# Attention's small products moved to TensorE's full tile size, with a new cost rule in the order planner

## The chip, the core and the metric

One core of one Trainium2 chip runs the whole program. The metric is the device time of one execution in microseconds (us). TensorE is the matrix engine (PE in the profile; its weight loads are listed apart, as PEld), DVE is VectorE, ACT is ScalarE, POOL is GpSimd, and SP issues most DMA transfers.

## The reference

Three layers follow each other; all data are float32.

```python
p_packed = sm_attn(p, k, v)          # 8 batches x 8 heads, 32 packed queries over 576 keys of 64
out = sm_attn(q, p_packed, p_packed) # 576 queries over the 32 packed rows
x = out.transpose(0, 2, 1, 3).reshape(4608, 512)
logits = x @ w_gate                  # 8 experts
# greedy: the largest logits first; each token goes to one expert, each expert takes 576 tokens
out[mask_e] = relu(x[mask_e] @ w1[e]) @ w2[e]
# then, for all tokens:
y = maximum(maximum(x @ w1, x @ w2), x @ w3) @ w_out
```

## The kernel before

The program has two parts. Each collects its operations in an `Order` object and then lets `run` write them out in an order that a planner works out with its own costs (`price`) and its own clock per engine. The planner always takes the operation that can start first; at equal start the lower `level` wins, then the earlier one collected. So the order on each engine's queue is fixed at build time; the chip follows it with semaphores. When the planner sees TensorE idle it calls `busy`, which puts dummy bf16 products (L562) in the gap: `int((us - GAP) * FILL / 0.22)` of them.

**Part one, attention.** For each of 8 batches `load` fetches keys (kt), values (v4, and the last 64 keys' values in v1), packed queries (pt) and queries (qt). Inside `pack`, for each of two groups of four heads: the packed logits `s` (stationary 128 rows x 64 columns), softmax, five transposes of `a1` (the fifth has 64 columns only), the product with the values into 32-row pieces (stationary 32 columns; the last chunk has only 64 contraction rows), two transposes, and `G`, the gate weights pulled through the packed values (stationary 64 columns). `query` then takes one or two tiles of 128 tokens: logits in pieces of 64 tokens (L521 to L523), softmax on DVE and ACT, transposes, and the gate logits in pieces of 32 tokens (L552 to L555) into `Lm`. `attend` multiplies the softmax with the block-diagonal packed values and stores a tile of 128 rows of x to memory (`x_dram`). Nine of the 36 tiles are attended in part one, 27 in part two.

A float32 product is recorded as two instructions on TensorE, so every count of such products in the profile is twice that of the code. The shape of the array that an instruction uses follows its operands: `128*64` in the profile is 128 contraction rows by 64 stationary columns, and products of a shape under 128 run side by side on different parts of the array.

`some` converts a piece of the last layer's weights from 64-bit words (`raw64`, `c64`, `w64`, `both64`) and writes it back to memory. It runs at level 30, that is, only where the planner finds nothing else to do. There are 18 pieces; 7 are collected into part one, the other 11 into part two (4 ahead of `gather(0)`, 7 later; all of them at level 30 and through the same two buffers).

**Part two, experts.** `epoch(k)` finds on DVE, with small products on TensorE, which expert fills next and which 576 tokens it takes (`idx`). `gather(k)` fetches their rows of `x_dram` with POOL's indirect DMA; it waits for the stores of all of x. Then the expert layers and the last layers follow for those tokens on TensorE. `epoch(0)` and the 27 attends come first; `epoch(k+1)` is planned beside expert k.

## Time and profile before

| what | value |
|---|---|
| median of 3 runs | 1273.7 us (1271.32 to 1274.76) |
| the profiled execution's own time | 1274.22 us |
| its span, first to last instruction | 1272.5 us |
| PE busy, share of the span | 1225.9 us, 96% |
| PEld busy | 1138.2 us, 89% |
| DVE busy | 778.4 us, 61% |
| ACT busy | 380.2 us, 30% |
| mean granted TensorE clock | 0.980 |
| one load of qt, of v4, of v1 | 1152, 1024 and 128 KB |

Times inside the execution are microseconds from the span's start. Busy time of PE contains the latency of its pipeline: the number of instructions that start in a stretch says more than the busy share. PEclk is the granted clock as a share of 2.4 GHz.

### The profile page before, as it was taken

Reading aid. Unit: us, or ns where it says so; the run is one execution under the profiler, and the core shown is the slowest. Engines: PE = TensorE matmul, PEld = TensorE weight load, DVE = VectorE, ACT = ScalarE, POOL = GpSimd, SP = SyncE. Lnnn points to the kernel's source line nnn. Section 1 sums busy time; section 2 is a strip of 40 time slices with the busy share of each in tenths; the row PEclk is TensorE's granted clock in tenths of the full one; section 3 lists DMA queues with packets and bytes.
Section 4 is the critical chain, followed back from the end, with each engine's and each line's share of the span. In section 5 each row is a group of like instructions: output and inputs, shape, how many; then the busy total and the mean of one; then the engine's idle time right before and its main releaser. Section 6 shows DMA issues by size and latency. Waiting matters only on the chain.

```text
span 1272.5 us, 25973 instructions
## 1 busy us (share of the span) xinstructions
PE 1225.9 (96%) x10396; PEld 1138.2 (89%) x10396; DVE 778.4 (61%) x2129; ACT 380.2 (30%) x849; POOL 85.2 (7%) x221
## 2 busy tenths in 40 slices
PE   8999877999899999999999999999999999999997
PEld 4667767999799989999999989998999899989995
DVE  4879789999889999999993522252225222432220
ACT  3445445334321233123312422133213221332121
POOL 1000001000301020001100020002000300010001
PEclk9999897999899999999999999999999999999999
DMA  9984485884426433443244224433443345323511
GB/s 342 363 317 166 152 275 187 261 273 130 133 85 214 120 114 99 134 142 108 91 149 157 85 100 142 151 97 117 142 153 98 114 133 166 92 75 100 166 34 42
DMA packets 70058, 191.50 MB, mean 150 GB/s; under 512 B 7729, under 2 KB 17969, under 8 KB 67889
## 3 DMA queue, kind: packets, MB, share of 16 engines
q1 hardware_dynamic: 63712, 169.89, 41.2%
q0 software_dynamic: 6080, 19.93, 4.7%
q8 instruction: 82, 1.34, 0.4%
q14 instruction: 40, 0.32, 0.1%
q10 hardware_dynamic: 144, 0.02, 0.0%
HBM read 161.50 MB, written 28.31 MB: 149 GB/s over the span
## 4 chain that ended last, share of the span: by engine, by line
PE 58%; issue 16%; DVE 4%; POOL 1%; DMA 1%; ACT 0%; POOLq 0%; DVEq 0%; ACTq 0%
PE mm L190 57%; POOL out_dram L867 1%; DMA xg<-x_dram,idx 1%; DVE R L190 1%; PE pst L190 1%; PE psr L190 1%; DVE act L190 0%; DVE t L190 0%; DVE hl L190 0%; DVE eq L190 0%; DVE val L190 0%; DVE m L190 0%; DVE pj L190 0%; DVE pos L190 0%; POOL xg L190 0%
## 5 line engine op out<-in xcount | busy, mean ns | idle before, releaser
L190 PE MATMUL mm<-act,hl 128*128 128x288 f32 x6528 | 886.4, 297 | 0.7 <-ACT act L190 0.6
L190 PEld LDWEIGHTS mm<-act,hl 128*128 128x128 f32 x6528 | 874.3, 189 | 2.1 <-ACT act L190 1.4
L190 DVE TENSOR_TENSOR t<-mm,t 128x288 f32<-128x288 f32 x192 | 87.5, 456 | 143.4 <-PE mm L190 143.1
L190 ACT ACTIVATE act<-mm 128x288 fp32r<-128x288 f32 (+1 forms) x208 | 81.4, 398 | 239.7 <-PE mm L190 233.8
L190 PE MATMUL mm<-WO,act 128*128 128x512 f32 x576 | 144.4, 401 | 0.0
L190 PEld LDWEIGHTS mm<-WO,act 128*128 128x128 f32 x576 | 103.9, 188 | 22.9
L190 ACT ACTIVATE hl<-raw 128x512 fp32r<-128x512 f32 x128 | 80.7, 633 | 120.0 <-PE mm L190 101.3
L190 DVE TENSOR_TENSOR hl<-raw,hl 128x512 fp32r<-128x512 f32 x128 | 87.6, 690 | 45.8 <-ACT hl L190 42.5
L190 ACT ACTIVATE act<-t 128x288 fp32r<-128x288 f32 x96 | 42.6, 443 | 208.9 <-DVE t L190 208.2
L190 DVE SCALAR_TENSOR_TENSOR act<-mm,act 128x288 fp32r<-128x288 f32 x128 | 58.0, 454 | 69.4 <-ACT act L190 69.2
L190 POOL DMA_INDIRECT xg<-x_dram,idx x40 | 41.4, 1035 | 701.2 <-PE pst L190 449.8
L190 DVE TENSOR_TENSOR act<-mm,act 128x288 fp32r<-128x288 f32 (+1 forms) x80 | 32.6, 422 | 88.6 <-ACT act L190 88.6
L190 ACT ACTIVATE osb<-mm 128x512 f32<-128x512 f32 x63 | 37.1, 599 | 120.4 <-PE mm L190 113.1
L867 POOL DMA_INDIRECT out_dram<-osb,idx x32 | 33.8, 1057 | 465.4 <-ACT osb L190 285.0
L190 DVE TENSOR_REDUCE ri<-R 128x30 int32<-128x1080 bf16 x48 | 61.2, 1275 | 0.8
L190 DVE TENSOR_TENSOR act<-t,act 128x288 fp32r<-128x288 f32 x96 | 43.8, 456 | 23.2 <-ACT act L190 23.0
L190 ACT ACTIVATE t<-mm 128x288 f32<-128x288 f32 x96 | 39.2, 409 | 57.5 <-PE mm L190 56.7
L190 DVE TENSOR_TENSOR R<-m,cand 128x540 bf16<-128x540 f32 (+1 forms) x63 | 36.3, 594 | 0.0
L190 DVE TENSOR_TENSOR R<-R,code 128x1080 bf16<-128x1080 bf16 x48 | 34.6, 720 | 0.9
L190 PE MATMUL mm<-act 128*128 128x128 f32 (+1 forms) x240 | 34.2, 301 | 0.9 <-DVE Lm L190 0.9
L190 PE MATMUL s<-kt,pt 128*64 128x288 f32 x128 | 29.4, 440 | 3.2 <-ACT a L190 3.2
L190 DVE TENSOR_TENSOR act<-pst,act 128x64 fp32r<-128x64 f32 (+1 forms) x60 | 24.2, 438 | 13.3 <-ACT act L190 13.1
(157 smaller groups left out, 910.7 us busy)
## 6 DMA issues: line engine op xcount, KB each, us to landing
hl<-W SPq DMA_DIRECT2D x144, 512.0 KB, 4.0
raw<-in_w_dram SPq DMA_DIRECT2D x128, 256.0 KB, 2.7
kt<-in_kT_dram SPq DMA_DIRECT2D x16, 576.0 KB, 8.5
qt<-in_qT_dram SPq DMA_DIRECT2D x8, 1152.0 KB, 9.8
raw<-in_w_dram SPq DMA_DIRECT2D x18, 512.0 KB, 5.9
W<-both SPq DMA_DIRECT2D x18, 512.0 KB, 4.7
v<-in_v_dram SPq DMA_DIRECT2D x8, 1024.0 KB, 9.7
x_dram<-osb SPq DMA_DIRECT2D x27, 256.0 KB, 4.3
```

The lines of the kernel that those rows point to most:

```text
L190: return self.add(eng, aps, cost, moved, lambda: getattr(engine, method)(*args, **kw), after)
L867: ins = nc.gpsimd.indirect_dma_start(out=out, out_offset=bass.IndirectOffsetOnAxis(ap=idx, axis=0), in_=osb, in_offset=None)
```

## The change

The queries' logits take all rows of a tile in one product (stationary up to 128 columns instead of 64); the gate logits do too (128 instead of 32). `G` is one product for both pairs of heads, with 16 moving columns, from which ScalarE copies the two useful blocks; before, two products and one DVE copy. The fifth transpose of `a1` takes the last 128 columns, so that the last value product has 128 contraction rows; the 64 rows that repeat are met by zeros that POOL writes into the lower half of v1. Three buffers for queries and values instead of two. The conversion pieces are collected per batch, 6 in place of 7 in part one and 5 in place of 4 ahead of `gather(0)` (18 in all, as before).

In the planner, a float32 product gets a new price, each change of the array's shape on TensorE costs 0.15 us, and at equal start and level the operation that needs no such change goes first. The gap filler takes smaller gaps and more of each. In `epoch`, `pd` and `val` are computed ahead of `nb`, `r` and `R1`.

```diff
-QTB = KTB = 2
-UNITS_A, UNITS_B = 7, 4
+QTB, KTB, VB = 3, 2, 3
+UNITS_A, UNITS_B = (0, 0, 1, 2, 2, 1, 0, 0), 5
-GAP, FILL = 0.6, 0.7
+GAP, FILL = 0.4, 0.8
+SWITCH = 0.15
...
-                return 4 * max(cols, k) / self.PE_SPEED * min(1.0, k / 128) * (1.12 if k < 128 else 1.0) + 0.022
+                wide = 32 if k <= 32 else 64 if k <= 64 else 128
+                return 2 * max(2 * cols, wide) / self.PE_SPEED * wide / 128 * (1.12 if k < 128 else 1.0) + 0.012
...
+    def turns(self, i):
+
+        return self.modes.get(i, self.mode) != self.mode
...
-                    can = sorted((s, ops[i][3], i) for i in c if (s := start(i)) is not None)
+                    can = sorted((s, (ops[i][3][0], self.turns(i), i), i) for i in c if (s := start(i)) is not None)
...
-            self.free[eng] = e = s + cost
+            self.free[eng] = e = s + cost + (SWITCH if self.turns(i) else 0.0)
+            self.mode = self.modes.get(i, self.mode)
...
-            V4[b] = o.tile(inp, [P, 4, DM], F32, "v4", 2)
+            V4[b] = o.tile(inp, [P, 4, DM], F32, "v4", VB)
             o.sp.dma_start(V4[b], v4[b])
-            V1[b] = o.tile(inp, [64, DM], F32, "v1", 2)
-            o.sp.dma_start(V1[b], v1[b])
+            V1[b] = o.tile(inp, [P, DM], F32, "v1", VB)
+            o.pool.memset(V1[b][:64], 0.0)
+            o.sp.dma_start(V1[b][64:], v1[b])
...
-                turn(t2[:64], a1[:, 512:])
+                turn(t2, a1[:, S - P:])
...
-                o.dve.tensor_copy(a1T[:64, 4], t2[:64])
+                o.dve.tensor_copy(a1T[:, 4], t2)
                 for c in range(5):
-                    w = min(P, S - c * P)
...
-                        o.pe.matmul(pp[32 * h:32 * h + 32, :64], a1T[:w, c, 32 * h:32 * h + 32],
+                        o.pe.matmul(pp[32 * h:32 * h + 32, :64], a1T[:, c, 32 * h:32 * h + 32],
...
+                o.pe.matmul(pp[:, 320:320 + 2 * E], PPT[b][:, 2 * g:2 * g + 2].rearrange("p a c -> p (a c)"),
+                            wg_sb[:, 2 * g:2 * g + 2].rearrange("p a e -> p (a e)"), start=True, stop=True)
                 for pr in range(2):
-                    o.pe.matmul(pp[64 * pr:64 * pr + 64, 320:320 + E], PPT[b][:, 2 * g + pr], wg_sb[:, 2 * g + pr],
-                                start=True, stop=True)
-                o.dve.tensor_copy(G[:, b, g], pp[:, 320:320 + E])
+                    rows = slice(64 * pr, 64 * pr + 64)
+                    o.act.activation(G[rows, b, g], pp[rows, 320 + E * pr:320 + E * pr + E], AF.Copy)
...
-                        for c in range(0, m, 64):
-                            o.pe.matmul(ps[r0 + c:r0 + c + 64, i, 64 * pr:64 * pr + 64], QT[b][:, pr, tok + c:tok + c + 64],
-                                        PPT[b][:, pr], start=True, stop=True)
+                        o.pe.matmul(ps[r0:r0 + m, i, 64 * pr:64 * pr + 64], QT[b][:, pr, tok:tok + m], PPT[b][:, pr],
+                                    start=True, stop=True)
...
-                    for c in range(0, m, 32):
-                        for g in range(2):
-                            o.pe.matmul(pl[r0 + c:r0 + c + 32, i * E:(i + 1) * E], aT[b][:, g, tok + c:tok + c + 32],
-                                        G[:, b, g], start=(g == 0), stop=(g == 1))
+                    for g in range(2):
+                        o.pe.matmul(pl[r0:r0 + m, i * E:(i + 1) * E], aT[b][:, g, tok:tok + m], G[:, b, g],
+                                    start=(g == 0), stop=(g == 1))
...
-        o.level = 0
-        some(work, UNITS_A)
+            o.level = 0
+            some(work, UNITS_A[b])
```

In `epoch` the five lines that make `pd` and `val` move, unchanged, from behind the loop that makes `R1` to a place ahead of `nb`.

## Rows read from the trace of the kernel before

**Rows 1.** Stretches of the span: stretch, length, busy us and instructions of each engine.

```profile
core 0: us, PE busy (x) PEld busy (x) DVE busy (x) ACT busy (x) POOL busy (x), PEclk, DMA share, GB/s
25.00:77.00 52.00, 49.19 (x948) 33.88 (x948) 43.78 (x137) 22.98 (x47) 0.00 (x0) 1.00 1.02 365
77.00:125.00 48.00, 45.41 (x873) 33.31 (x874) 40.09 (x121) 22.16 (x45) 0.00 (x0) 0.96 0.64 220
125.00:138.00 13.00, 8.82 (x238) 6.87 (x234) 12.67 (x43) 5.50 (x11) 0.00 (x0) 0.84 0.11 43
138.00:179.00 41.00, 40.27 (x523) 36.72 (x524) 31.24 (x127) 18.04 (x32) 0.00 (x0) 0.93 0.67 232
...
331.00:341.00 10.00, 6.74 (x34) 4.28 (x33) 8.43 (x18) 3.00 (x5) 2.06 (x2) 0.89 0.27 101
```

**Rows 2.** Waits of the weight loads, 0 to 143 us: total us, times, longest.

```profile
PEld bank L190 <- issue: 15.7, 43, 1.8
```

**Rows 3.** Timeline of weight loads around 127 us: start, us, count, idle before.

```profile
126.61 0.42 PEld L190 LDWEIGHTS bank<-eye,a 128*128 128x128 f32 x4 [0.61 <-issue]
127.20 1.01 PEld L190 LDWEIGHTS bank<-ppt,qt 128*64 128x64 f32 x30 [0.17 <-issue]
128.27 0.38 PEld L190 LDWEIGHTS bank<-G,act 128*32 128x32 f32 x32
128.67 0.20 PEld L190 LDWEIGHTS bank<-ppt,qt 128*64 128x64 f32 x4
```

**Rows 4.** Groups of weight loads by shape, 0 to 146 us.

```profile
L190 PEld LDWEIGHTS bank<-ppt,qt 128*64 128x64 f32 x576 | 22.7, 140 | 5.6 <-issue 4.4
...
L190 PEld LDWEIGHTS bank<-G,act 128*32 128x32 f32 x576 | 8.3, 116 | 9.3 <-issue 4.7 <-ACT act L190 3.2 <-ACT e L190 0.6
...
L190 PEld LDWEIGHTS bank<-eye,a 128*64 128x64 f32 x16 | 1.8, 114 | 2.0 <-issue 1.3 <-DVE c L190 0.4 <-ACT a1T L190 0.2
```

**Rows 5.** Timeline: runs of full-width weight loads in three stages.

```profile
19.41 0.20 PEld L190 LDWEIGHTS bank<-eye,act 128*128 128x128 f32 x2 [0.44 <-DVE act L190]
...
162.95 0.97 PEld L190 LDWEIGHTS mm<-act 128*128 128x128 f32 x8
...
398.92 2.15 PEld L190 LDWEIGHTS mm<-act,hl 128*128 128x128 f32 x16
```

**Rows 6.** Groups of DVE instructions, 0 to 146 us: busy us, mean ns.

```profile
L190 DVE TENSOR_SCALAR c<-c 128x512 f32<-128x512 f32 (+1 forms) x14 | 5.8, 417 | 0.2 <-ACT c L190 0.2
L190 DVE SCALAR_TENSOR_TENSOR w<-raw,c 128x512 int32<-128x512 int32 x7 | 4.8, 686 | 0.0
...
L190 DVE COPY G<-bank 128x8 f32<-128x8 f32 x16 | 2.6, 159 | 3.6 <-PE bank L190 3.5
```

**Rows 7.** Groups of ACT instructions, 0 to 210 us.

```profile
L190 ACT ACTIVATE act<-pst 128x64 fp32r<-128x64 f32 x4 | 0.6, 232 | 0.7 <-PE pst L190 0.7
```

**Rows 8.** Timeline where part one ends, 138 to 146 us.

```profile
138.28 7.89 PEld L190 LDWEIGHTS mm<-act 128*128 128x128 f32 x48 [1.03 <-DVE Lm L190]
...
139.36 0.42 DVE L190 TENSOR_SCALAR c<-w 128x512 int32<-128x512 int32 x1
...
145.34 0.69 DVE L190 TENSOR_TENSOR both<-w,both 128x512 fp32r<-128x512 f32 x1 [0.70 <-ACT both L190]
145.95 0.42 DVE L190 TENSOR_SCALAR eq<-who 128x288 f32<-128x288 bf16 x1
```

**Rows 9.** Timeline of epoch 0's end and the gather, 183 to 191 us.

```profile
183.51 1.36 SPq L190 DMA_DIRECT2D x_dram<-osb  x3
...
185.04 0.53 DVE L190 TENSOR_TENSOR val<-tk,pd 128x360 bf16<-128x360 bf16 x1
...
185.62 0.76 PE L190 MATMUL psr<-val,R 128*128 128x40 bf16 x18 [4.53 <-DVE val L190]
...
187.45 0.16 DVE L190 CAST idx<-psr 128x5 int32<-128x5 f32 x1 [0.20 <-PE psr L190]
...
190.41 1.21 POOL L190 DMA_INDIRECT xg<-x_dram,idx  x1 [184.00 <-DMA raw<-in_w_dram]
```

More of the change, by code (lines that the diff above doesn't have):

```diff
@@ L75, in __init__ @@
         self.level, self.pe_level, self.filler = 0, None, None
+        self.mode = None
         self.free = dict.fromkeys(("pe", "dve", "act", "pool", "sp", "dma"), 0.6)
@@ L81, in reset @@
         self.ops, self.seen, self.touch = [], {}, {}
+        self.modes = {}
         self.queue_of = {}
@@ L189, in trace @@
             cost, moved = self.price(eng, method, aps, kw), 0
-        return self.add(eng, aps, cost, moved, lambda: getattr(engine, method)(*args, **kw), after)
+        me = self.add(eng, aps, cost, moved, lambda: getattr(engine, method)(*args, **kw), after)
+        if eng == "pe":
+            lhs = next(x for x, write in aps if not write)
+            self.modes[me] = tuple(32 if n <= 32 else 64 if n <= 64 else 128
+                                   for n in (int(lhs.shape[0]), int(np.prod([int(d) for d in lhs.shape[1:]]))))
+        return me
     @staticmethod
@@ L753, in epoch @@
                             op=OP.is_ge)
+        pd = T([P, NT, 10], BF, "pd")
+        o.dve.tensor_tensor(pd, pj[:, :, :10], pj[:, :, 1:], op=OP.subtract)
+        val = T([P, NT, 2, 5, 2], BF, "val")
+        for h in range(2):
+            o.dve.tensor_tensor(val[:, :, h], tk[:, :, None, :].to_broadcast([P, NT, 5, 2]),
+                                 pd[:, :, h:10:2][:, :, :, None].to_broadcast([P, NT, 5, 2]), op=OP.mult)
         nb = T([P, NT], F32, "nb")
@@ L760, in epoch @@
                                 r[:, c:c + 12, None].to_broadcast([P, 12, 64]), op=OP.is_equal)
-        pd = T([P, NT, 10], BF, "pd")
-        o.dve.tensor_tensor(pd, pj[:, :, :10], pj[:, :, 1:], op=OP.subtract)
-        val = T([P, NT, 2, 5, 2], BF, "val")
-        for h in range(2):
-            o.dve.tensor_tensor(val[:, :, h], tk[:, :, None, :].to_broadcast([P, NT, 5, 2]),
-                                 pd[:, :, h:10:2][:, :, :, None].to_broadcast([P, NT, 5, 2]), op=OP.mult)
         pi = R()
```

## The prediction

> **What bounds the kernel now.** I read the stretches of the span first, to see which engine sets each stage, then the waits, the timeline at the seams, and the groups for prices. From 25 to 125 us TensorE is busy 94.6 of 100 us, DVE 83.9, and the DMA engines are full only up to 77 us [rows 1]. But TensorE's busy time holds little work: its weight loads stand idle 15.7 us before products into a bank with nothing that the profile shows [rows 2]. The timeline says where: inside a run the loads follow closely, between runs of two shapes there is a hole [rows 3]. From 125 to 138 us DVE takes over: 12.67 of 13 us busy, while TensorE falls to 8.82 and its granted clock to a mean of 0.84 [rows 1]. From 138 us TensorE attends the 27 tiles that are left, at first slowly: 48 loads in 7.89 us [rows 8], 164 ns each, where the same loads later take (0.97 - 0.14) / 7 = 119 ns at most [rows 5]. DVE, meanwhile, finishes conversion pieces from 139.36 to 145.95 us before epoch 0 can begin [rows 8]. At the far end the token indices are there at 187.45 + 0.16 us, yet the gather starts at 190.41; the last three stores of x were issued at 183.51 to 184.87 [rows 9]. So the stores, behind TensorE's attends, come last there, and DVE's epoch 2.8 us before them. From there to the end the experts run on a full TensorE, which the change does not touch but through the planner.
>
> So what is to be gained is how much earlier the attends can start, and how fast they run.
>
> **The change part by part.**
>
> *Shape changes on TensorE.* Out of the four full-width transposes, the last load starts at about 126.61 + 0.42 - 0.14 = 126.89 us and the first 64-column load at 127.20: 0.31 us, against 0.11 within the run, so 0.20 us for the change. From 32 columns back to 64: 128.27 + 0.38 - 0.11 = 128.54 to 128.67, 0.13 us against 0.01, so 0.12 us [rows 3]. The Trainium skill, TensorEngine Tiling (Array Packing), Key Properties, has the reason: a change of tiling mode, not of tile, drains TensorE; it gives no price, the trace does. How many changes go: the 64-column transpose among full ones, 16 times in and out [rows 4] = 32; the value chunk of 64 rows, 16; the gate products, 16; from the code, 20 query calls whose logits and gate logits each go into a small shape and out, 80. That is 144 at most; where a small-shape neighbour stays (the packed logits `s`, the 32-column value products, the four tiles that straddle two batches) nothing is saved. I take 100 at 0.15 us: -15 us. Bounds: 60 x 0.12 = -7, 140 x 0.20 = -28.
>
> *Queries.* 32 of 36 tiles lie in one batch: 512 of the 576 loads become 256 of 128 columns. The old ones follow at (1.01 - 0.14) / 29 = 30 ns [rows 3]: 15.4 us. The trace has no full-width float32 load before 64 moving columns. From below: two full-width loads start 0.20 - 0.14 = 0.06 us apart [rows 5], which is also twice the 30 ns at which two half-width products run side by side. From above: 110 ns, the run of transposes and attends [rows 3, 5], which have 128 moving columns, twice as many. I take 65 ns, since the expert products show a load hidden under its predecessor's 288 columns at 134 ns [rows 5]: 16.6 us, +1.2 (0 to +12.8).
>
> *Gate logits.* 512 loads at (0.38 - 0.11) / 31 = 8.7 ns [rows 3] = 4.5 us become 128; at 65 ns 8.3 us, +3.8 (+3.2 to +9.6). Alone, this part loses; it pays only through its shape changes. `G` itself: 64 loads become 32, zero within 1 us either way.
>
> TensorE's net: -15 + 1.2 + 3.8 = -10 us, between -24 and +15.
>
> *DVE.* The copies of `G` go: 16 x 0.159 = -2.5 us. One piece fewer in part one: 2 x 0.417, four like the 0.686, one more like the first, -4.0 us [rows 6]. Conversion is collected batch by batch, but it keeps level 30 and its own buffers, and no other operation has that level: as far as I can see the spreading itself alters nothing in the plan, only the count does. The piece that goes to part two costs DVE 4.0 us there; it is covered by the 9.8 us that DVE idles between 138 and 179 us [rows 1] and by the 6.6 us of leftovers that no longer stand ahead of epoch 0. Uncovered it would be +4.
>
> *ACT and POOL.* 32 copies for `G`, nearest row 0.232 us [rows 7]: 7.4 us on an engine that is busy 45 of 100 us there [rows 1]; hidden, and 7.4 us on the path if every one were waited for. POOL's eight zero fills: no row is near; by DVE's 512 columns, 0.69 us each, 5.5 us as an upper estimate; POOL is idle from 25 to 179 us [rows 1] and the third buffer gives a batch of lead. Zero.
>
> *Third buffers.* Values and queries of batch 2, 2.3 MB, now go to SP's queue ahead of batch 2's keys, which at 365 GB/s [rows 1] come 6.3 us later. The batch is complete after the same number of bytes, and the queries then need not wait for a buffer. Zero, with up to +6 if DVE has nothing else then (it idles 8.2 us in 25 to 77 us as it is).
>
> *`val` ahead of `R1`.* The 18 products now wait 4.53 us for `val` [rows 9]; afterwards two thirds could run under the making of `R1`: at most 0.5 us, on a chain that the stores of x outlast. Zero.
>
> *Fillers.* More dummy products in smaller gaps keep the clock up over 125 to 138 us, unless they delay real ones. The slow 48 loads cost 48 x 0.054 = 2.6 us; I take half, -1.3.
>
> *Sum.* The attends start when the last gate logits are through, which DVE sets. It loses 2.5 us of work, and gets back part of its idle time, 16.5 us from 25 to 138 us, since the engine that it waits for is 10 us lighter: I take half of those 10. That is -7.4 us (0 to -12.5), and with the clock -8.7. The gather needs the attends' stores, so this passes through to the experts. Epoch 0 gains more (its leftovers go as well) and stays ahead. From 1274.2 us of the profiled execution, 1265.5; its time is 0.5 us above the median shown, so 1265.
>
> The experts' order is planned anew with shifted clocks. It has one soft place, 331 to 341 us, where TensorE is busy 6.74 of 10 us before expert 1's gather [rows 1]: +-3 us, taken as zero.
>
> **The rivals.**
>
> *The loads are not hidden.* Each full-width float32 load costs what it does in the attends, 110 ns. Then 384 loads take 42.2 us in place of 19.9, and less the 15 us of shape changes TensorE is 7.4 us heavier; DVE waits for it, and the time goes to about 1280. It decides from (15 + 19.9) / 384 = 91 ns a load. For it: no run in the trace is closer than that. Against: the pair 0.06 us apart. A rule speaks for this rival: the Trainium skill, TensorE: Matmul & The Clock Gate, LDWEIGHTS (loading the stationary operand), has a load take its columns over 1.2 in ns, 107 ns for 128 columns, whatever moves; by that I estimate 384 x 107 = 41 us and a time of 1279. The pair disagrees with it.
>
> *The gain is given back.* TensorE gets lighter but DVE, over 97% busy at the end of part one, starts the attends only its own 2.5 us earlier, or the epoch with its extra piece, or the new order at 331 us, eats the rest: 1271 to 1276. For it: DVE from 77 to 138 us is busy 52.8 of 61 us. Against: 8 us of that stretch are idle, and epoch 0 has 6.6 us of slack to come.
>
> *All of it counts.* DVE's idle time is all recovered, the clock holds, and the order at 331 us improves: 1274.2 - 12.5 - 2.6 - 3 = 1256.
>
> **How the numbers follow.** The forecast 0.61 (its own range 1258 to 1269), given back 0.21, loads not hidden 0.13, all of it 0.05. A measurement of this kernel tells about 0.3%, 3.8 us, from no change. So faster 0.66, same 0.21, slower 0.13. The range of 8 in 10 reaches from 1256 to 1277: below lies half of the last case, above the unhidden loads.
>
> **What would show it.** Right: the first attend near 131 us; full-width query loads 60 to 70 ns apart; the unexplained 15.7 us more than halved; DVE free of conversion when the last gate logits are copied; the gather near 182 us, and the expert part as long as before. Wrong: query loads 90 ns or more apart; the first attend at 138 us with DVE full up to it; a gather that waits for the indices in place of the stores; or a wider hole around expert 1's gather.

## The result and the profile after

| | median us | range | against the kernel before |
|---|---|---|---|
| before, beside it | 1274.08 | 1271.32 to 1274.76 (4 runs) | |
| changed | 1288.79 | 1286.96 to 1293.61 (4 runs) | 1.0125 [1.0094, 1.0157], slower by 1.2%, clear of noise |

The forecast was 1265 us, the range 1256 to 1277. The profile shown here is of the slowest of the four executions (1293.61 us, span 1291.8). Two of e13's ten executions ran in a slower state and are left out of its median below.

First the stretches of the changed kernel, in the columns of [rows 1]; from 138 us on the cuts follow its own stages.

```profile
core 0: us, PE busy (x) PEld busy (x) DVE busy (x) ACT busy (x) POOL busy (x), PEclk, DMA share, GB/s
25.00:77.00 52.00, 49.93 (x568) 39.72 (x564) 35.85 (x105) 23.48 (x55) 1.56 (x3) 0.93 0.97 349
77.00:125.00 48.00, 46.67 (x573) 36.89 (x571) 38.94 (x118) 21.07 (x51) 0.52 (x1) 0.93 0.54 193
125.00:138.00 13.00, 12.65 (x190) 11.17 (x189) 10.45 (x34) 5.58 (x16) 0.00 (x0) 1.00 0.11 42
138.00:150.00 12.00, 10.75 (x82) 8.32 (x81) 10.53 (x34) 5.00 (x10) 0.00 (x0) 0.98 0.12 46
...
339.00:361.00 22.00, 16.79 (x68) 12.66 (x68) 18.41 (x56) 5.09 (x12) 7.57 (x7) 0.69 0.39 131
```

From 25 to 125 us TensorE is busier than before (96.6 of 100 us against 94.6) with far fewer instructions (1138 against 1818 in the 100 us taken as one), and its weight loads rise from 67.2 to 76.6 us. DVE, which was to gain, falls from 83.9 to 74.8 busy us: its waits for TensorE in these 100 us rise from 14.5 to 23.4 us. The granted clock is lower too, 0.93 against 0.98. The last row is a hole of 22 us which before was a soft place of 10.

The timeline of the changed kernel's weight loads (start, us, count) gives the price that the forecast had to guess.

```profile
90.22 0.97 PEld L194 LDWEIGHTS bank<-ppt,qt 128*128 128x128 f32 x8
91.50 0.97 PEld L194 LDWEIGHTS bank<-G,act 128*128 128x128 f32 x8
...
130.76 0.97 PEld L194 LDWEIGHTS bank<-G,act 128*128 128x128 f32 x8 [0.15 <-ACT act L194]
131.65 0.97 PEld L194 LDWEIGHTS bank<-ppt,qt 128*128 128x128 f32 x8
```

Eight loads in 0.97 us, the last of them 0.19: (0.97 - 0.19) / 7 = 111 ns from load to load, for 64 moving columns (ppt) as for 8 (G). Between all neighbours of one run up to 158 us the median distance is 112 ns for the queries and 111 to 112 for the gate logits. None of the load time is hidden. This is the pace at the full clock; where the granted clock stood at the lower of its two levels (1.2 GHz), from 36.8 to 43.6 us, the same loads follow at 213 ns.

The groups of its weight loads, in the form of [rows 4], give the counts:

```profile
L194 PEld LDWEIGHTS bank<-ppt,qt 128*128 128x128 f32 x256 | 32.8, 200 | 1.0 <-issue 0.4
L194 PEld LDWEIGHTS bank<-G,act 128*128 128x128 f32 x128 | 16.3, 195 | 0.9 <-ACT act L194 0.8
```

256 x 0.112 = 28.7 us in place of the 15.4 of the 64-column loads, 128 x 0.112 = 14.3 in place of 4.5: TensorE pays 23 us. On the other side the unexplained waits of [rows 2] fall from 15.7 to 6.5 us (waits of the weight loads, 0 to 155 us):

```profile
PEld bank L194 <- issue: 6.5, 22, 0.9
```

In the sequence of the loads, the changes of the array's shape go from 176 (to 143 us, where part one ends) to 107 (to 160 us), and the distances from load to load across them, each counted up to 0.3 us, from 42.0 to 28.4 us. So TensorE gains 13.6 and pays 23.2: about 10 us heavier, where the forecast had it 10 us lighter.

The seam between the parts, on the timeline, as in [rows 8]:

```profile
150.38 7.89 PEld L194 LDWEIGHTS mm<-act 128*128 128x128 f32 x48 [0.43 <-DVE Lm L194]
151.46 0.68 DVE L194 TENSOR_TENSOR w<-w,c 128x512 f32<-128x512 f32 x1
...
156.29 0.69 DVE L194 TENSOR_TENSOR both<-w,both 128x512 fp32r<-128x512 f32 x1 [0.70 <-ACT both L194]
156.90 0.42 DVE L194 TENSOR_SCALAR eq<-who 128x288 f32<-128x288 bf16 x1
```

The attends start at 150.4 us (before: 138.3), DVE still has 5.5 us of conversion ahead of epoch 0, and the attends start as slowly as before, 48 loads in 7.89 us in both. In both the granted clock is at its lower level there, first the changed kernel, then the kernel before (stretches, in the columns above):

```profile
149.40:156.20 6.80, 6.47 (x31) 6.37 (x31) 5.32 (x15) 1.20 (x3) 0.00 (x0) 0.50 0.20 80
133.90:144.10 10.20, 8.85 (x113) 8.30 (x114) 9.70 (x32) 1.53 (x4) 0.00 (x0) 0.50 0.13 53
```

At epoch 0's end, as in [rows 9]:

```profile
194.48 0.85 SPq L194 DMA_DIRECT2D x_dram<-osb  x2
196.11 0.32 PE L194 MATMUL psr<-val,R 128*128 128x40 bf16 x6 [0.55 <-DVE R L194]
197.41 0.16 DVE L194 CAST idx<-psr 128x5 int32<-128x5 f32 x1
201.83 1.12 POOL L194 DMA_INDIRECT xg<-x_dram,idx  x1 [113.28 <-DMA W<-both]
```

The indices are ready at 197.57 and the gather starts at 201.83: the last store lands at 200.6, so as before it is the stores that come last, and the gather stands 11.4 us later than in [rows 9].

Expert 1's tokens then come later still. On the timelines of the kernel before (L190) and of the changed one (L194), DVE's copy that makes the indices and, right behind it, the gather:

```profile
322.72 0.16 DVE L190 CAST idx<-psr 128x5 int32<-128x5 f32 x1
323.15 1.18 POOL L190 DMA_INDIRECT xg<-x_dram,idx  x1 [1.13 <-DVE idx L190]
338.43 0.15 DVE L194 CAST idx<-psr 128x5 int32<-128x5 f32 x1
338.86 1.04 POOL L194 DMA_INDIRECT xg<-x_dram,idx  x1 [2.13 <-DVE idf L194]
```

Here it is the indices that come last, 15.7 us later than before. In the hole of the stretch 339 to 361 TensorE waits for the tokens, on the timeline:

```profile
347.59 0.37 PE L194 MATMUL pst<-eye,xg 128*128 128x128 f32 x1 [1.84 <-DMA xg<-x_dram,idx]
```

Expert 0's last layer starts 11.1 us later than before, expert 1's 19.2 later (475.4 against 456.2). From there to the end every kernel of this study takes 815 to 818 us. So all of the loss lies ahead of 476 us: the profiled executions differ by 1293.61 - 1274.22 = 19.4 us.

So two paths lead into the experts. The stores of x set expert 0. DVE's epochs, one behind the other, set expert 1: in all eighteen kernels expert 1's last layer starts 132 to 137 us behind its indices, though these come anywhere from 305 to 346 us, and the indices come 135 to 150 us behind expert 0's. From expert 0's last layer to expert 1's it is 134 to 136 us where there is hardly a hole (e3, e6, e9, e12, e13, e14), 142.4 in the kernel before and 150.5 in the changed one. A late epoch 0 therefore reaches the end even where, as at the first gather, the stores outlast it.

### The profile page after: what moved, and what is told of

Its sections match the earlier page's. It is cut to its first block, busy times and chain, and to the rows that moved or that the text cites. A ratio compares the mean times of both kernels' runs of the same rounds, so it can differ in the third digit from the quotient of the medians.

```text
span 1291.8 us, 24638 instructions
## 1 busy us (share of the span) xinstructions
PE 1249.3 (97%) x9712; PEld 1164.8 (90%) x9712; DVE 777.7 (60%) x2113; ACT 385.3 (30%) x881; POOL 88.0 (7%) x229
## 4 chain that ended last, share of the span: by engine, by line
PE 75%; issue 12%; DVE 9%; DMA 2%; POOL 1%; ACT 1%; POOLq 0%; DVEq 0%; ACTq 0%
PE mm L194 63%; PE bank L194 8%; PE s L194 2%; PE psr L194 1%; DVE R L194 1%; DMA xg<-x_dram,idx 1%; PE pst L194 1%; DVE act L194 1%; DVE c L194 1%; DVE t L194 1%; DVE hl L194 1%; POOL out_dram L880 1%; DMA raw<-in_wo_dram 1%; PE wp L575 0%; POOL xg L194 0%
## 5 line engine op out<-in xcount | busy, mean ns | idle before, releaser
L194 PE MATMUL mm<-act,hl 128*128 128x288 f32 x6528 | 893.0, 298 | 0.8 <-ACT act L194 0.7
L194 PEld LDWEIGHTS mm<-act,hl 128*128 128x128 f32 x6528 | 877.4, 189 | 2.7 <-ACT act L194 1.7
L194 DVE TENSOR_TENSOR t<-mm,t 128x288 f32<-128x288 f32 x192 | 87.3, 455 | 148.2 <-PE mm L194 147.1
L194 ACT ACTIVATE act<-mm 128x288 fp32r<-128x288 f32 (+1 forms) x208 | 81.2, 398 | 246.6 <-PE mm L194 246.4
L194 PE MATMUL mm<-WO,act 128*128 128x512 f32 x576 | 144.5, 401 | 0.0
L194 PEld LDWEIGHTS mm<-WO,act 128*128 128x128 f32 x576 | 104.1, 188 | 22.7
L194 ACT ACTIVATE hl<-raw 128x512 fp32r<-128x512 f32 x128 | 80.7, 632 | 125.3 <-PE mm L194 102.2
L194 DVE TENSOR_TENSOR hl<-raw,hl 128x512 fp32r<-128x512 f32 x128 | 87.7, 688 | 45.4 <-ACT hl L194 41.8
L194 ACT ACTIVATE act<-t 128x288 fp32r<-128x288 f32 x96 | 42.4, 442 | 215.5 <-DVE t L194 214.9
L194 DVE SCALAR_TENSOR_TENSOR act<-mm,act 128x288 fp32r<-128x288 f32 x128 | 57.9, 453 | 69.9 <-ACT act L194 69.9
L194 DVE TENSOR_TENSOR act<-mm,act 128x288 fp32r<-128x288 f32 (+1 forms) x80 | 32.5, 419 | 89.6 <-ACT act L194 89.4
L194 POOL DMA_INDIRECT xg<-x_dram,idx x40 | 40.9, 1022 | 635.7 <-PE pst L194 450.7
L194 ACT ACTIVATE osb<-mm 128x512 f32<-128x512 f32 x63 | 37.2, 598 | 115.4 <-PE mm L194 106.0
L194 DVE TENSOR_REDUCE ri<-R 128x30 int32<-128x1080 bf16 x48 | 61.1, 1273 | 0.8
L194 DVE TENSOR_TENSOR act<-t,act 128x288 fp32r<-128x288 f32 x96 | 43.6, 454 | 23.6 <-ACT act L194 23.5
L194 ACT ACTIVATE t<-mm 128x288 f32<-128x288 f32 x96 | 39.1, 407 | 55.5 <-PE mm L194 53.5
L194 PE MATMUL bank<-ppt,qt 128*128 128x64 f32 (+1 forms) x320 | 39.3, 277 | 0.0
L194 PEld LDWEIGHTS bank<-ppt,qt 128*128 128x128 f32 (+1 forms) x320 | 35.9, 191 | 1.9 <-issue 0.9
L194 DVE TENSOR_TENSOR R<-m,cand 128x540 bf16<-128x540 f32 (+1 forms) x63 | 36.2, 593 | 0.0
L194 DVE TENSOR_TENSOR R<-R,code 128x1080 bf16<-128x1080 bf16 x48 | 34.5, 719 | 0.9
L194 PE MATMUL mm<-act 128*128 128x128 f32 (+1 forms) x240 | 34.4, 301 | 0.3 <-DVE Lm L194 0.3
```

The lines of the kernel that those rows point to most:

```text
L194: me = self.add(eng, aps, cost, moved, lambda: getattr(engine, method)(*args, **kw), after)
```

## The experiments

Four theories were put against each other. A: the full-width loads take 112 ns each and nothing hides them. B: the planner prices a full-width float32 product at 0.119 us (it has two loads, so 0.224 on the chip) and puts the work into an order that counts on time that is not there. C: the pieces, the buffers or the shape rule. D: the third buffers delay batch 2's keys. "The kernel before" in each row ran beside the experiment.

| run | median us | ratio to the kernel before |
|---|---|---|
| e1_small_pieces | 1270.19 | 0.9966 [0.9952, 0.9979] |
| e2_full_tiles_alone | 1277.07 | 1.0025 [0.9998, 1.0053] |
| e3_true_price | 1279.06 | 1.0037 [1.0020, 1.0053] |
| e4_seven_pieces | 1295.77 | 1.0154 [1.0120, 1.0188] |
| e5_full_tiles_low_price | 1290.81 | 1.0133 [1.0113, 1.0153] |
| e6_small_two_buffers | 1265.20 | 0.9939 [0.9920, 0.9959] |
| e7_keys_and_gate_alone | 1269.48 | 0.9972 [0.9956, 0.9988] |
| e8_third_buffers_alone | 1281.11 | 1.0067 [1.0042, 1.0091] |
| e9_gate_logits_full | 1260.50 | 0.9914 [0.9895, 0.9933] |
| e10_queries_full | 1290.64 | 1.0142 [1.0110, 1.0174] |
| e11_no_shape_rule | 1280.32 | 1.0059 [1.0042, 1.0075] |
| e12_third_keys | 1266.66 | 0.9958 [0.9941, 0.9975] |
| e13_same_order_queries | 1268.89 | 0.9970 [0.9944, 0.9995] |
| e14_same_order_gate | 1267.60 | 0.9955 [0.9940, 0.9970] |
| e15_before_order_full | 1286.83 | 1.0117 [1.0073, 1.0161] |
| e16_changed_order_small | 1277.17 | 1.0032 [1.0014, 1.0050] |

### e1: the changed kernel with the small pieces back

```diff
-                        o.pe.matmul(ps[r0:r0 + m, i, 64 * pr:64 * pr + 64], QT[b][:, pr, tok:tok + m], PPT[b][:, pr],
-                                    start=True, stop=True)
+                        for c in range(0, m, 64):
+                            o.pe.matmul(ps[r0 + c:r0 + c + 64, i, 64 * pr:64 * pr + 64], QT[b][:, pr, tok + c:tok + c + 64],
+                                        PPT[b][:, pr], start=True, stop=True)
...
-                    for g in range(2):
-                        o.pe.matmul(pl[r0:r0 + m, i * E:(i + 1) * E], aT[b][:, g, tok:tok + m], G[:, b, g],
-                                    start=(g == 0), stop=(g == 1))
+                    for c in range(0, m, 32):
+                        for g in range(2):
+                            o.pe.matmul(pl[r0 + c:r0 + c + 32, i * E:(i + 1) * E], aT[b][:, g, tok + c:tok + c + 32],
+                                        G[:, b, g], start=(g == 0), stop=(g == 1))
```

> The changed kernel with its query products back in pieces of 64 tokens and its gate logits back in pieces of 32; everything else of the change stays. Theory A (each full-width float32 load takes 112 ns, not hidden: 256 query loads and 128 gate loads cost 43 us where the small ones cost 20): the first attend of part two moves from 150 us to 125 to 135 us, the time falls to 1262 to 1272 us, below the kernel before. Theory B (the new planner price, 0.119 us for a product that the chip does in 0.224, spoils the order): the same direction, since the small pieces are priced about rightly, so this run alone does not part A from B. Theory C (third buffers, one piece more in part two, the new planner rule): the time stays above 1280 us.

1270.2, 18.6 us below the changed kernel and 4.0 below the kernel before. The first attend comes at 134.9 us, epoch 0 at 136.2 with no conversion left ahead of it, expert 1's indices at 317.0. So the two full-width products, with the order that follows from them, are the whole loss and more; the rest of the change is a gain.

### e2: the kernel before with the full-width products alone

The diff of e1 the other way round, on the kernel before; its planner prices such a product at 0.235 us.

> The kernel before with only the query products and the gate logits at full tile size; planner, price (0.235 us for such a product, about what the chip takes), buffers and pieces as before. Theory A: TensorE gets 23 us of loads more and saves 40 to 80 shape changes of 0.15 us, so 10 to 17 us are lost: 1283 to 1291 us, first attend at 147 us or later. Theory B: with the right price the order is good, 1270 to 1278 us. Theory C: no change, 1271 to 1277 us.

1277.1, or +2.9 us with an interval that just reaches no change. The attends start at 146.6 us, 8.3 later, of which the end keeps a third. Its stretch from 25 to 125 us:

```profile
25.00:125.00 100.00, 99.37 (x1277) 77.13 (x1276) 89.32 (x271) 43.85 (x91) 0.00 (x0) 1.00 0.82 290
```

TensorE is full, as A has it; but DVE does 89.3 us of work there, against 83.9 before and 74.8 in the changed kernel, and nothing is left for it ahead of epoch 0 (147.8 us, 1.8 later than before). Expert 1's indices come 5.4 us later than before, not 8.3. With the loads alone the kernel loses little: something else costs the other 12 us.

### e3: the changed kernel with the product's measured price

```diff
-                return 2 * max(2 * cols, wide) / self.PE_SPEED * wide / 128 * (1.12 if k < 128 else 1.0) + 0.012
+                return 2 * max(2 * cols, 2 * wide if wide == 128 else wide) / self.PE_SPEED * wide / 128 * (1.12 if k < 128 else 1.0) + 0.012
```

The planner then reckons 0.225 us for a full-width product; the instructions are the same, the dummy products aside (25 instead of 40).

> The changed kernel whose planner prices a full-width float32 product by its two loads of 128 columns (0.225 us in place of 0.119). Theory A: the work on TensorE is the same, 1283 us or more. Theory B: the order mends, 1276 us or less. Theory C: 1283 us or more.

1279.1: 9.7 us back, by one number in a planner, between the ranges of A and B. Part one and the start of epoch 0 in e3 (stretch, then timeline):

```profile
25.00:125.00 100.00, 99.03 (x1264) 79.49 (x1264) 88.16 (x256) 48.48 (x118) 2.07 (x4) 0.99 0.76 278
```

```profile
145.03 0.17 DVE L194 COPY Lm<-bank 128x8 f32<-128x8 f32 x1 [0.26 <-PE bank L194]
...
146.53 0.42 DVE L194 TENSOR_SCALAR eq<-who 128x288 f32<-128x288 bf16 x1
```

TensorE starts 1264 instructions in place of 1138, DVE does 88 us of work in place of 75 (its waits for TensorE fall from 23.4 to 9.9 us), and the 5.5 us of conversion between the last gate logits and epoch 0 are gone. Expert 0's last layer starts no earlier for it (325.7 us against 324.9). The gain comes by the other path: epoch 0 starts 10.4 us earlier, expert 1's indices are there at 325.7 us, 12.7 earlier, and expert 1's last layer starts at 460.5 in place of 475.4.

### e5: e2 with the changed kernel's price

```diff
-                return 4 * max(cols, k) / self.PE_SPEED * min(1.0, k / 128) * (1.12 if k < 128 else 1.0) + 0.022
+                wide = 32 if k <= 32 else 64 if k <= 64 else 128
+                return 2 * max(2 * cols, wide) / self.PE_SPEED * wide / 128 * (1.12 if k < 128 else 1.0) + 0.012
```

> The kernel with full tiles alone (1277.1 us), and in its planner only the changed kernel's price for float32 products, which charges a full-width one 0.119 us where the chip takes 0.224. Theory B (a price that is too low by 20 us in sum spoils the order): 5 to 12 us slower than with the true price, 1282 to 1289 us, DVE less busy from 25 to 125 us than the 89.3 us of the run with the true price. Theory A (only the loads themselves cost): 1275 to 1280 us.

1290.8, 13.7 above e2 and 2 above B's range, with none of the other edits in it. (The new formula also moves the other float32 prices, by 0.01 to 0.04 us each; that of the full-width queries and gate logits falls by 0.116.) Its stretch shows the same signature as the changed kernel's:

```profile
25.00:125.00 100.00, 97.33 (x1187) 74.44 (x1190) 77.49 (x237) 42.52 (x88) 0.00 (x0) 0.98 0.81 283
```

DVE 77.5 where e2 has 89.3 (waits for TensorE 17.5 us where e2 has 8.2), epoch 0 at 159.6 where e2 has 147.8, expert 1's indices at 344.1 against 328.1. B holds from both sides: +9.7 and +13.7. The granted clock is a rival for the first of these, since from 25 to 125 us it is 0.93 in the changed kernel and 0.99 in e3; for the second it is not, with 0.98 in e5 and 1.00 in e2.

### e4: a seventh piece in part one

```diff
-UNITS_A, UNITS_B = (0, 0, 1, 2, 2, 1, 0, 0), 5
+UNITS_A, UNITS_B = (0, 0, 1, 2, 3, 1, 0, 0), 4
```

> The changed kernel with 7 conversion pieces in part one and 11 in part two, as in the kernel before. Theory C in its form that the twelfth piece makes DVE late for expert 1's gather: 4 to 8 us faster than the changed kernel, 1281 to 1285 us, and idle time of TensorE around expert 1's gather back to 6 us. Theory A alone: within 3 us of 1289 us, since part one is bound by TensorE and DVE has room there.

1295.8, 7 above the changed kernel: the missing piece was not its loss, and C in this form falls. Both expected ranges were missed. Where the 7 us arise can be read from the trace: DVE has 8.4 us of conversion work between the last gate logits and epoch 0, where the changed kernel has 4.6, and epoch 0 starts at 163.7 us in place of 156.9.

### e6, e8 and e12: the buffers

e6 is e1 with two buffers each for queries, keys and values; e12 is e6 with three for the keys (2, 3, 2 in the line below); e8 is the kernel before with three for queries and values.

```diff
-QTB, KTB, VB = 3, 2, 3
+QTB, KTB, VB = 2, 2, 2
```

```diff
-QTB = KTB = 2
+QTB, KTB = 3, 2
...
-            V4[b] = o.tile(inp, [P, 4, DM], F32, "v4", 2)
+            V4[b] = o.tile(inp, [P, 4, DM], F32, "v4", 3)
...
-            V1[b] = o.tile(inp, [64, DM], F32, "v1", 2)
+            V1[b] = o.tile(inp, [64, DM], F32, "v1", 3)
```

> The changed kernel with small pieces back (1270.2 us) and two buffers for queries and values in place of three. Theory D (the third buffers put batch 2's values and queries ahead of its keys; batch 2's packing began at 45 us there and at 36 us in the kernel before): packing of batch 2 at 34 to 38 us, 3 to 6 us faster, 1264 to 1267 us. Rival (the third buffers pay later, when queries need not wait for a buffer): 1272 to 1277 us.

> The kernel before with three buffers for queries and values in place of two, nothing else. Theory D: batch 2's packing later than 36 us by 4 to 9 us, time 1276 to 1280 us. Rival (third buffers pay): 1268 to 1272 us.

> The kernel with small pieces, two buffers for queries and values, and three for keys. Theory D turned round (what comes early in SP's queue should be what packing needs first): batch 2's packing starts before 34 us and the time is 1260 to 1264 us. Rival (DVE is full anyway, so earlier keys give nothing): 1264 to 1268 us.

e6 1265.2 (5.0 below e1 by the medians; the intervals just overlap), e8 1281.1 (7.9 above the kernel before by the medians, 8.5 by the ratio). What is late is seen in e8's stretches and on the timeline of its SP queue:

```profile
25.00:60.00 35.00, 31.55 (x542) 22.26 (x541) 26.74 (x83) 14.44 (x31) 0.00 (x0) 1.00 1.03 374
60.00:70.00 10.00, 8.29 (x130) 6.31 (x132) 3.36 (x11) 3.08 (x6) 0.00 (x0) 0.55 1.03 399
70.00:125.00 55.00, 53.80 (x1156) 38.53 (x1153) 50.71 (x160) 25.74 (x54) 0.00 (x0) 0.99 0.54 192
```

```profile
10.76 3.07 SPq L190 DMA_DIRECT2D v<-in_v_dram  x2
13.88 0.59 SPq L190 DMA_DIRECT2D qt<-in_qT_dram  x1
15.12 1.80 SPq L190 DMA_DIRECT2D raw<-in_w_dram  x2
...
25.97 1.77 SPq L190 DMA_DIRECT2D kt<-in_kT_dram  x2
```

With a free third buffer batch 2's values and queries are issued at 10.8 to 14.5 us; its keys, whose buffers are still two, at 26.0, where the kernel before issued them at 18.4. They land at 35.1 and 36.5 us instead of 29.3 and 32.4, batch 2's packing starts at 41.7 instead of 35.9, and from 60 to 70 us DVE does 3.4 of 10 us, with the granted clock at a mean of 0.55. D holds for the packing. It does not hold for the way to the end: the last gate logits are through at 136.3 us and the attends start at 136.6, earlier than before (138.1 and 138.3). But DVE has 10.1 us of conversion work left ahead of epoch 0, where the kernel before has 5.9, so epoch 0 starts 3.6 us later (149.5) and expert 1's indices come 5.0 later. e12 shows that a third buffer for the keys alone brings nothing (1266.7, the rival's range; packing at 36.7 against e6's 34.5, not before 34): two are enough here.

### e7: the last keys and the gate weights alone

The kernel before with the diff's lines for `V1`, `t2`, `a1T` and `G`, and nothing else.

```diff
-                turn(t2[:64], a1[:, 512:])
+                turn(t2, a1[:, S - P:])
...
+                o.pe.matmul(pp[:, 320:320 + 2 * E], PPT[b][:, 2 * g:2 * g + 2].rearrange("p a c -> p (a c)"),
+                            wg_sb[:, 2 * g:2 * g + 2].rearrange("p a e -> p (a e)"), start=True, stop=True)
...
-                o.dve.tensor_copy(G[:, b, g], pp[:, 320:320 + E])
+                    o.act.activation(G[rows, b, g], pp[rows, 320 + E * pr:320 + E * pr + E], AF.Copy)
```

> The kernel before with only the last keys in a full transpose and a value product of 128 rows, the gate weights in one product and their copies on ScalarE; planner and the rest as before. If shape changes are what these parts save: some 48 to 60 changes of 0.15 us, 7 to 9 us of TensorE, and 2.5 us of DVE, of which half reaches the end: 1267 to 1271 us. Rival (DVE and its leftover conversion set the end of part one, so a lighter TensorE gives nothing): 1272 to 1276 us.

1269.5: -3.7 us. The attends start at 131.4, epoch 0 at 141.0. Here full width takes a shape out of the sequence and adds next to no load time (32 loads of `wg_sb` at 109 ns in place of 64 short ones), so only the gain is left.

### e11: no charge for a change of shape

```diff
-        return self.modes.get(i, self.mode) != self.mode
+        return False
```

in e6, so that the planner neither pays for a change nor prefers an operation without one.

> The kernel with small pieces and two buffers (1265.2 us), with a planner that neither charges changes of the array's shape nor prefers operations without one. If the rule is what makes the order good: 1268 to 1274 us, and more than 180 changes in part one where that kernel has 171. Rival (the rule is worth nothing, the gain over the kernel before comes from the last keys and the gate): 1262 to 1267 us.

1280.3, 15.1 above e6 and above both ranges: the rule is the best part of the change. But not by the number of changes, as expected of it: up to the first attend of part two e11 has 147 of them, e6 144. DVE does 85.8 us of work in the stretch from 25 to 125 us against 90.6, and the planner put in 48 dummy products. In the profiled executions, 20.1 us apart, expert 0's last layer starts 6.0 us later than in e6, and the other 14 us are a hole ahead of expert 1's tokens (148.8 us from last layer to last layer against 134.4). Why the order without the rule makes the epochs late stays open.

### e9 and e10: one full-width product each, at the measured price

e6 with the price of e3 and the gate logits (e9) or the queries' logits (e10) at full width.

The edit of e9 beside that price (e10's is the other half of the diff of e1, turned round):

```diff
-                    for c in range(0, m, 32):
-                        for g in range(2):
-                            o.pe.matmul(pl[r0 + c:r0 + c + 32, i * E:(i + 1) * E], aT[b][:, g, tok + c:tok + c + 32],
-                                        G[:, b, g], start=(g == 0), stop=(g == 1))
+                    for g in range(2):
+                        o.pe.matmul(pl[r0:r0 + m, i * E:(i + 1) * E], aT[b][:, g, tok:tok + m], G[:, b, g],
+                                    start=(g == 0), stop=(g == 1))
```

> The kernel with small pieces and two buffers (1265.2 us), its gate logits alone back at full tile size, priced by their true 0.225 us. Theory A with the trace's numbers (128 loads at 112 ns for 512 at 8.7: +9.9 us of TensorE, less what shape changes it saves, at most 40 of 0.15 us): 2 to 8 us slower, 1267 to 1273 us. Rival (shape changes pay for the loads): 1262 to 1266 us.

> The kernel with small pieces and two buffers (1265.2 us), its query products alone back at full tile size, priced by their true 0.225 us. Theory A (256 loads at 112 ns for 512 at 30: +13.3 us of TensorE, less at most 40 shape changes of 0.15 us): 3 to 10 us slower, 1268 to 1275 us. Rival (shape changes pay for the loads): 1262 to 1267 us.

e9 has the lowest median of the study, 1260.5 us, under both expected ranges; its interval overlaps that of e6. Its stretch has DVE at 96.2 of 100 us, the fullest of all:

```profile
25.00:125.00 100.00, 97.05 (x1571) 76.18 (x1570) 96.17 (x288) 53.74 (x128) 2.65 (x5) 1.00 0.79 288
```

Part two's first attend is at 130.0 us and expert 1's indices at 305.3. e10 fell to 1290.6, 25 above e6 and outside both ranges, far more than its 13 us of loads. Its stretch 100 to 150 us and, on the timelines of TensorE and ACT, the end of part one:

```profile
100.00:150.00 50.00, 40.05 (x575) 33.15 (x574) 33.84 (x97) 15.74 (x33) 0.00 (x0) 0.89 0.23 83
```

```profile
141.60 2.88 PE L194 MATMUL bank<-act 128*64 128x128 f32 x16 [0.39 <-DVE Lm L194]
148.65 1.22 PE L194 MATMUL mm<-act 128*128 128x128 f32 x4 [4.17 <-ACT xs L194]
144.52 1.57 ACT L194 ACTIVATE xs<-bank 128x512 f32<-128x512 f32 x3 [3.78 <-PE bank L194]
147.52 1.09 ACT L194 ACTIVATE xs<-bank 128x512 f32<-128x512 f32 x2 [1.42 <-DMA x_dram<-xs]
```

TensorE idles 10 us in that stretch: the plan put ACT's copies (xs) of five of part one's nine attended tiles behind the last attend's products, and part two's first attend waits 4.17 us for the last of them. The granted clock, too, is at its lower level from 139.3 to 156.3 us. The waits are the order's, not a price of the chip; the next runs hold the order fixed.

### e13 to e16: the same order, other products

In these the planner sees one kernel's operations and the engine is given another's: the first piece issues the whole full-width product and the others nothing (e13 queries, e14 gate logits, both in e6's order; e15 both, in the order of the kernel before), or the full-width product issues its pieces (e16, in the changed kernel's order).

```diff
+                            one = lambda b=b, tok=tok, r0=r0, m=m, c=c, i=i, pr=pr: None if c else nc.tensor.matmul(
+                                ps[r0:r0 + m, i, 64 * pr:64 * pr + 64], QT[b][:, pr, tok:tok + m], PPT[b][:, pr],
+                                start=True, stop=True)
+                            o.instead = one
...
+        me = self.add(eng, aps, cost, moved, self.instead or (lambda: getattr(engine, method)(*args, **kw)), after)
```

> The kernel with small pieces and two buffers (1265.2 us), planned with the small pieces, so that every engine's order stays, but each query product is issued once at full tile size where its first piece stood. What is left is the price of the loads themselves: 256 at 112 ns for 512 at 30, +13.3 us of TensorE less the shape changes that go. Theory A: 4 to 13 us slower, 1269 to 1278 us. Theory B (the 25 us that the replanned kernel lost were the order's): 1265 to 1270 us, and far under 1290 us in either case.

> The same for the gate logits alone: the order of the kernel with small pieces and two buffers (1265.2 us), each gate product issued once at full tile size in place of its first piece. Theory A: +9.9 us of TensorE less shape changes, 1267 to 1273 us. Theory B (the 5 us that the replanned kernel gained are the order's): no gain here, 1265 us or more. Rival (full gate logits are cheaper in themselves): 1258 to 1263 us.

> The order of the kernel before, word for word, with queries and gate logits issued at full tile size. Theory A: +23 us of loads less the shape changes that go (at most 80 of 0.15 us): 1280 to 1292 us. The replanned kernel with the same products took 1277 us; Theory B has this one slower than that, since here the plan counts the pieces' price. Rival (loads hidden): 1268 to 1276 us.

> The order of the changed kernel, word for word, with each full query and gate product issued as its small pieces at the same place. The pieces take about the 0.12 us that the planner charged for the full product, so now the plan is true. Theory B (the loss comes from a plan that counts on times that the chip does not keep): 1264 to 1275 us. Rival (that order is bad in itself): 1280 us or more.

e13 +3.7 over e6 by the medians, just under A's range and in B's, and e14 +2.4, in A's range; the intervals of both overlap that of e6. e15 is 13.4 over the kernel before, clear of noise. In e15 the loads are 23 us longer and 48 changes of shape go (199 to 151 up to 163 us; at 0.15 us each, 7 us; by the distances across them, 12 us): 11 to 16 us net on TensorE, and 13.4 arrive. That is A with the order held, but not with the plan true: e2, the same products replanned at about their price, runs 9.8 us faster. Nor was the clock held; it is at its lower level from 129.5 to 156.8 us in e15, from 133.9 to 144.1 in the kernel before. e13, where the stretch that e10 spoiled has TensorE at 46 us instead of 40, shows that e10's other 22 us came with its order:

```profile
100.00:150.00 50.00, 46.16 (x779) 39.97 (x778) 43.23 (x141) 22.57 (x49) 0.00 (x0) 1.00 0.38 134
```

e16 gives the changed kernel's plan about the time that it counted on: a pair of 64-column pieces takes 4 x 0.030 = 0.12 us, the planned price of the full product. It runs in 1277.2, 11.6 below the changed kernel, with the very same order: A once more, between the two expected ranges. Yet it stays 7.0 above e1, which has the same operations and an order of its own. Its expert 0 is as early as e1's (last layer at 310.7 and 311.9 us); the rest is the hole ahead of expert 1's tokens, 147.2 us from last layer to last layer against 137.8.

## Why the prediction was wrong, point by point

The mechanism that decided was a named rival, "the loads are not hidden", held at 0.13; and the loss went beyond its 1280, because two more steps failed with it: the planner's order and the path to expert 1.

**Queries and gate logits: the step that failed.** "I take 65 ns" was the price of both; measured: 111 to 112 ns, just above the upper bound. +13.3 us in place of +1.2, and +9.9 in place of +3.8. Against 110 ns stood one pair of loads 0.06 us apart [rows 5]. That pair (`eye,act`) is a transpose, not a product with few moving columns. In the traces of both kernels, up to 175 us, the first two loads of a run of transposes start 56 to 65 ns apart where the loads stood idle just before, and 76 ns or more where they did not; the first two of a run of full-width products start at least 108 ns apart, idle or not. First a pair of the kernel before, of an attend, then a transpose's and two products' (gate weights, gate logits) of the changed one:

```profile
106.79 0.30 PEld L190 LDWEIGHTS bank<-act 128*128 128x128 f32 x2
88.94 0.20 PEld L194 LDWEIGHTS bank<-eye,act 128*128 128x128 f32 x2 [0.44 <-DVE sm L194]
20.81 0.30 PEld L194 LDWEIGHTS bank<-wg_sb,ppt 128*128 128x128 f32 x2 [0.44 <-DVE ppt L194]
95.94 0.30 PEld L194 LDWEIGHTS bank<-G,act 128*128 128x128 f32 x2
```

A product's load takes 0.19 us, so 0.30 - 0.19 = 0.11 us; a transpose's 0.14, so 0.06. The run of eight products in [rows 5] said the same: with 0.19 in place of the 0.14 that the forecast subtracted, (0.97 - 0.19) / 7 = 111 ns and not "119 ns at most". The Trainium skill, TensorE: Matmul & The Clock Gate, LDWEIGHTS (loading the stationary operand), gives a load's time as its columns over 1.2 in ns, so 107 for 128 columns, with no term for what moves. These traces agree within 5% at the full clock, with 8, 16, 64 and 128 moving columns.

**The planner's order: "+-3 us, taken as zero" failed too.** The price was part of the diff and was read as bookkeeping. It is worth 9.7 us (the changed kernel against e3) and 13.7 (e5 against e2), because the forecast's own mistake stands in it: the planner takes the full product as hidden, at 0.119 us. Its plan counts on some 20 us of TensorE that are not there: 192 products (half of the 384 loads) at 0.105 us too little. DVE pays from 25 to 125 us, in its waits for TensorE: 23.4 us against 9.9 in e3, 17.5 in e5 against 8.2 in e2. It then has conversion left ahead of epoch 0, and the delay reaches the end by expert 1's indices.

**The path.** "The gather needs the attends' stores, so this passes through to the experts. Epoch 0 gains more [...] and stays ahead" holds for expert 0. The sum has no term for expert 1, whose gather waits for DVE's epochs, in the kernel before too; the hole at 331 to 341 us was seen and put at zero. Of the 19.4 us between the profiled executions 11.1 stand at expert 0's last layer, 8.1 more come behind it, ahead of expert 1's.

**Third buffers: "Zero, with up to +6 if DVE has nothing else" was the wrong end.** +7.9 alone (e8), +5.0 in the changed kernel's company (e1 against e6). The order of the queue had been read rightly, keys behind 2.3 MB of values and queries; that "the batch is complete after the same number of bytes" missed that packing begins with the keys. Batch 2 is packed 5.8 us later in e8; by the end of part one the queries have caught up, and what is late is DVE's conversion and epoch 0 behind it.

**Shape changes: right in size.** -13.6 us measured against -15; fewer changes went (69, not 100) and each was worth more. "The unexplained 15.7 us more than halved" came true with it, at 6.5.

**DVE, ACT, POOL.** The `G` copies and the last keys bring the expected sort of gain (e7, -3.7). Whether "the spreading itself alters nothing in the plan" no run tests. That the leftovers ahead of epoch 0 would go did not: DVE, starved earlier, still had 5.5 us of them. They go in e1, e2, e3 and e6, where it is not starved.

**`val` and the fillers: small, as said.** With 40 dummy products in place of 20 the clock stood at 1.00 from 125 to 138 us (before: 0.84), but the slow start of the attends that this should have cured stayed: 48 loads in 7.89 us, 164 ns each. The clock fell later instead, from 149.4 to 156.2 us, just where the attends start.

**The sum.** e1 (everything but the full tiles) 1270.2; + 8.9 for the full tiles at the measured price (e3); + 9.7 for the low price = 1288.8. Split by the order instead, the same 18.6 us are 7.0 for the changed kernel's order (e16 against e1) and 11.6 for the full tiles in it (the changed kernel against e16); the two causes overlap, and no split is the only one. In e1 the third buffers are another +5.0. Of the forecast's list of what would show it wrong, two came as named, loads over 90 ns apart and a wider hole around expert 1's gather. The first attend came later than named, at 150 us, but with DVE at 10.5 of 12 us and not full; and the gather still waits for the stores.

**What stays open.** Orders made anew differ by several us for reasons that no run isolates: the gate logits cost 2.4 us in e6's order (e14) and gain 4.7 in their own (e9), both within overlapping intervals; e10 loses 22 us more than e13; e16 stays 7.0 above e1. The trace says where such losses stand, mostly ahead of expert 1's tokens, not why the planner's order makes them. The stretches at the lower clock differ from kernel to kernel as well and were not held fixed. A single term under some 5 us cannot be read from the total of a replanned kernel.

## What to carry to other kernels

Take the pace of an instruction from a long run of its own kind, never from a pair of another kind (here a transpose's), and where no run matches, from the nearest product whose operand the engine must load in full: with few moving columns a full-width float32 product costs its two loads, and small pieces side by side can be the cheaper form. Where an order is made by a planner, a wrong price is a second cost on top of the work itself, here as large as the first: put the measured duration in before judging an edit. A deeper buffer for one operand lets it overtake another in a shared queue, so ask first which operand the next stage starts with. And where a later stage hangs on a second path, put that path into the sum as well: here the first gather hid an epoch that was late for the second.

## What the runs showed of the hardware that was not expected

- At the full clock full-width float32 loads follow at 111 to 112 ns whether 8, 64 or 128 columns move, and at 108 to 112 in the pairs with 16 (`wg_sb`); at the lower of the two clock levels at 213 ns. Loads of 64 columns that run side by side follow at 30 ns and of 32 columns at 8.7 [rows 3]: a tile of 128 tokens' gate logits takes 4 x 112 = 0.45 us in full width and 16 x 8.7 = 0.14 us in pieces.
- The loads of transposes can start closer: the first two of a run 56 to 65 ns apart where the loads stood idle just before, the later ones 109 to 110 (median). The first two of a run of full-width products start at least 108 ns apart, idle or not.
- A change of the array's shape costs 0.12 to 0.20 us [rows 3], enough that 69 changes fewer paid for 13.6 of the 23.2 us that the slower loads cost.
- In e8 the granted clock has a mean of 0.55 from 60 to 70 us, near the lower of its two levels (1.2 GHz), although TensorE shows 8.3 us busy there. From 58 to 61.1 us, just before it fell, TensorE was busy 1.3 of 3.1 us.
